# Attention on one Trainium2 core: block moves in a VectorE form with an accumulator, and five buffers in place of three

## The chip, the cores and the metric

The kernel runs on one core of a Trainium2 chip. The metric is the time of one execution in microseconds (us) of device time. The engines of the core work side by side and each takes its own instructions in order: TensorE (PE, with its weight loads shown as PEld), VectorE (DVE), ScalarE (ACT), GpSimd (POOL) and SyncE (SP, which issues the DMAs here). They wait for one another through semaphores.

## The reference

Softmax attention without a mask, for 16 x 32 = 512 heads; each head has 192 queries and 1024 keys of 128 elements, all in bf16.

```python
B, H, Sq, Sk, D = 16, 32, 192, 1024, 128
def reference(q, k, v):
    scale = q.shape[-1] ** -0.5
    scores = jnp.einsum("bhqd,bhkd->bhqk", q, k) * scale
    p = _softmax(scores, axis=-1)
    return jnp.einsum("bhqk,bhkd->bhqd", p, v)
```

## The kernel before, in words

The 512 heads are taken in 128 quads of four heads; x counts quads. A quad has three steps, so there are 384 steps (f for the scores, s for the outputs, which run four steps behind: LAG = 4). Per step PE makes a third of the scores of the quad (`qk`, L612) and then a third of the outputs of the quad before (`pv`, L631).

What the engines do for a quad:

- SP loads K (1 MB, into `f_kn`), Q (0.19 MB, `f_qn`) and V (1 MB, `f_vs`), L505, L511 and L519, three buffers each (`NKN`, `NVS`), and stores two quads of outputs at a time (L531).
- DVE transposes K in three pieces into `f_kx` (`turn_k`, L697) and Q into `f_qt` (`turn_q`, L706), in blocks of 32 x 32.
- POOL puts the transposed K in order, in three copies, into `f_kt` (`order`, L570), and copies V in two halves into `f_vp` (`spread`, L579), where each row of 128 elements has a column of ones behind it. `f_kt` and `f_vp` have two buffers.
- PE multiplies K by Q into PSUM (`f_s`), ACT takes exp of it into `f_pt` (L788 and L791), PE multiplies that by V into PSUM (`f_o`); the column of ones gives the sum of the row.
- DVE divides (`onorm`): the reciprocal of the sums (L718), then the product with the outputs (L723).

`f_o` is a single PSUM bank. `pv(s)` therefore takes the semaphore `f_on` once (L627, through `take`, L596), which the product of `onorm(s - 1)` raises: PE cannot begin a step's outputs before DVE has divided those of the step before.

In every second quad (odd x) the first step is "wide" (`wide`, L496): its matmuls have 128 columns of weights instead of two times 64, so the outputs lie on other partitions than the store wants. `onorm` of a wide step writes into a scratch tile `f_ow`, and four moves of 64 partitions x 128 elements (L735) bring the blocks into `f_ob`. One move stands behind the `onorm` of the first step after the wide one, one behind the second, two behind the third (L729). The order on DVE is written out by hand, L758 to L769: per step f, `onorm(f - 5)` with its moves, then `turn_q` where one is due, then `turn_k(f + 5)`.

The order on SP is written out as well, L536 to L555. Per round n it loads K and Q of quad n + 3, then V of quad n + 1, then stores if a store is due. A load of K waits until DVE has transposed the quad that was in the buffer (`f_kx`, L504); a load of V waits for the second of the three output steps of the quad three before (`f_pv`, L518).

POOL takes, per quad, the three copies of K of quad x and then the two of V of quad x - 1 (L584). A copy of V waits for V's landing and for PE to be done with the buffer of `f_vp` that it overwrites (L577, L578).

A second, general path (`_general_path`) runs only if a sum of exponentials left its range; with these inputs it does not.

Of the kernel before, what the change touches and what calls it, by code (L numbers as in the profile page):

```python
# [6 lines left out]
F32 = mybir.dt.float32  # L7
ACT_FN = mybir.ActivationFunctionType
ALU = mybir.AluOpType
# [388 lines left out]
U32 = mybir.dt.uint32  # L398
# [9 lines left out]
def _attention_kernel(nc, q, k, v, out):  # L408
# [4 lines left out]
    NQ = NH // 4  # L413
# [3 lines left out]
    assert NH % 8 == 0 and NQ >= 12  # L417
    NF = 3 * NQ
    LAG = 4
    NKN, NVS, NKT, NVP = 3, 3, 2, 2  # L420
    GQ = 2
    NSO = 3
    VB = 130
# [9 lines left out]
    with ExitStack() as outer:  # L433
# [26 lines left out]
        with ExitStack() as es:  # L460
            def sb(name, shape, dt):
                return es.enter_context(nc.sbuf_tensor(name, shape, dt))
# [15 lines left out]
            pt = sb("f_pt", [128, R, 4, T * SQ], BF16)  # L478
            ob = sb("f_ob", [128, NSO, GQ * 6, D], BF16)
            ow = sb("f_ow", [128, 2, D], BF16)  # L480
            rinv = sb("f_rinv", [128, 2 * NF], F32)
            chk = sb("f_chk", [128, 2 * NF], F32)
            bad = sb("f_bad", [128, 2], BF16)
# [7 lines left out]
            def o_of(s):  # L491
                if NF - 4 <= s < NF - 1:
                    return s3_ps[0][:, s - (NF - 4), :].rearrange("p (u c) -> p u c", u=2)
                return o_ps[:]

            def wide(s):  # L496
                x, i = divmod(s, 3)
                return i == 0 and x % 2 == 1

            @block.sync  # L500
            def _(e):
                def load_k(x):
                    if x >= NKN:
                        e.wait_ge(s_kx, 3 * (x - NKN) + 3)  # L504
                    e.dma_start(  # L505
                        kn[:, x % NKN, :],
                        kf[4 * x:4 * x + 4].rearrange("a (j r) d -> (a j) (r d)", r=32).bitcast(U32),
                    ).then_inc(s_kn[x % NKN], 16)

                def load_q(x):  # L510
                    e.dma_start(  # L511
                        qn[:, x % NKN, :],
                        qf[4 * x:4 * x + 4].rearrange("a (j u) d -> (a j) (u d)", u=6).bitcast(U32),
                    ).then_inc(s_qn[x % NKN], 16)

                def load_v(x):
                    if x >= NVS:
                        e.wait_ge(s_pv, 3 * (x - NVS) + 2 + LAG)  # L518
                    e.dma_start(  # L519
                        vs[:, x % NVS, :, :],  # L520
                        vf[4 * x:4 * x + 4].rearrange("a (m t) d -> m a (t d)", t=T),
                    ).then_inc(s_v[x % NVS], 16)

                def store(i):
                    so = i % NSO
                    x, c = stores[i]
                    if x + c == NQ:
                        e.wait_ge(s_fin, 1)
                    else:
                        e.wait_ge(s_rc, 3 * (x + c) + 2)  # L530
                    e.dma_start(  # L531
                        of[4 * x:4 * x + 4 * c].rearrange("(a x) (p j) d -> (x p) a (j d)", x=2, j=3),
                        ob[:, so, 0:6 * c, :].rearrange("p (a j) d -> p a (j d)", j=3),
                    ).then_inc(s_st[so], 16)

                load_k(0)  # L536
                load_q(0)
                load_k(1)
                load_q(1)
                load_v(0)  # L540
                load_k(2)
                load_q(2)
                si = 0
                for n in range(NQ + 3):
                    if n + NKN < NQ:
                        load_k(n + NKN)
                        load_q(n + NKN)
                    if n + 1 < NQ:
                        load_v(n + 1)
                    if si < len(stores) - 2 and n >= sum(stores[si]) + 2:  # L550
                        store(si)
                        si += 1
                while si < len(stores):
                    store(si)
                    si += 1  # L555
                for so in range(NSO):
                    e.wait_ge(s_st[so], 16 * len(range(so, len(stores), NSO)))
# [121 lines left out]
            def _(dve):  # L679
# [31 lines left out]
                def onorm(s):  # L711
                    x, w = divmod(s, 3)
                    i, a = where[x]
                    so = i % NSO
                    ri = rinv[:, 2 * s: 2 * s + 2]
                    dve.wait_ge(s_pv, s + 1 + LAG)
                    O = o_of(s)
                    dve.reciprocal(ri, O[:, :, 128]).then_inc(s_rc, 1)  # L718
                    dve.wait_ge(s_rc, s + 1)
                    if a == 0 and w == 0 and i >= NSO:  # L720
                        dve.wait_ge(s_st[so], 16 * (i // NSO))
                    dst = ow[:] if wide(s) else ob[:, so, 6 * a + 2 * w: 6 * a + 2 * w + 2, :]
                    dve.tensor_tensor(  # L723
                        dst,
                        O[:, :, 0:128],
                        ri.unsqueeze(2).to_broadcast([128, 2, D]),
                        ALU.mult,
                    ).then_inc(s_on if s < NF - 1 else s_fin, 1)
                    for back, parts in ((1, (0, 1, 2, 3)),) if s == NF - 2 else ((1, (0,)), (2, (1,)), (3, (2, 3))):  # L729
                        if s == NF - 1 or s < back or not wide(s - back):  # L730
                            continue
                        i, a = where[(s - back) // 3]
                        for part in parts:
                            z, y = divmod(part, 2)
                            dve.tensor_copy(  # L735
                                ob[64 * z: 64 * z + 64, i % NSO, 6 * a + y, :].bitcast(U32),
                                ow[64 * y: 64 * y + 64, z, :].bitcast(U32))

                cnt = [0]

# [17 lines left out]
                for f in range(NF + LAG + 1):  # L758
                    s = f - LAG - 1
                    if s >= 0:  # L760
                        onorm(s)
                        if 0 <= s - EARLY < 3:
                            check(0, 2 * EARLY, 0, s - EARLY)
                    g = f + 5
                    if g < NF:
                        x, b = divmod(g, 3)
                        if b == 2 and x >= 2:
                            turn_q(x)
                        turn_k(g)  # L769
# [26 lines left out]
def bass_standalone__mha_softmax__near_ridge_kernel(  # L796
    nc: bass.Bass,
    q: bass.AP,
    k: bass.AP,
    v: bass.AP,  # L800
    out: bass.AP,
):
    _attention_kernel(nc, q, k, v, out)
# [28 lines left out]
```

## Time and profile before

| | |
|---|---|
| time, median of 3 runs (lowest to highest) | 870.58 us (866.5 to 877.46) |
| the profiled execution: time, span | 875.82 us, 871.8 us |
| granted TensorE clock, mean over the span | 0.99 |
| L735, the moves: count, busy, mean of one | 256, 110.2 us, 430 ns |
| L579, POOL's copies of V: count, mean of one | 256, 1044 ns |
| loads of K, V and Q, issue to landing, median | 10.9, 9.6 and 10.9 us |

The profile is of one execution. Its span runs from the first to the last instruction of the program; the time of the execution is a little longer. Lines are named as L735, line 735 of the kernel. In the list of waits a row has the engine, its tile and line, then behind the arrow what ended the wait, then the total in us, how often, and the longest. PEq is PE's sequencer, the part that takes the instructions and waits for semaphores, and SPq that of SP; "issue" is time in which an engine waited for nothing that the profile shows. In the groups of instructions a row has line, engine, operation, out<-in, sizes (partitions x elements), the count, then busy us, mean ns of one, and the idle time of the engine just before them with what ended it. In the timeline a row has start, length, engine, line, what it does, how many in a row, and in brackets the idle time before it. In the rows of DMA queues the share is the time that packets took on 16 DMA engines.

### The profile page before, as it was taken

To read this page: it belongs to the slowest core of one execution; us is meant where nothing else is said; L and a number is where in the kernel's file an instruction comes from. 1 tells how busy PE (TensorE), PEld (TensorE's weight loads), DVE (VectorE), ACT (ScalarE), POOL (GpSimd) and SP (SyncE) were. 2 spreads that over 40 slices of the span, in tenths; PEclk is the share of its full clock that TensorE was granted. 3 is DMA by queue.
4 is the path that set the end of the run, shared out by engine and by line. 5 is a ranking of instruction groups with operands and counts; after the bars stand their busy time and mean duration, and the time that the engine had idled before them with its cause. 6 is when DMAs were issued, how large, how long until landed. Compare 5 with 4: busy or idle time off the path is not lost. (4 is left out here: it accounts for less than half of the span.)

```text
span 871.8 us, 69465 instructions
## 1 busy us (share of the span) xinstructions
PE 828.7 (95%) x31882; PEld 737.8 (85%) x31882; DVE 707.3 (81%) x1544; ACT 753.2 (86%) x770; POOL 562.5 (65%) x646
## 2 busy tenths in 40 slices
PE   7899999999999999999999999999999999999995
PEld 4788888888888888888889888888888888888885
DVE  5488888888888888888888888888888888888874
ACT  4698988999898889998889888988888888888884
POOL 7466666676666666766666766666666666666661
PEclk9899999999999999999999999999999999999998
DMA  9799999999999999999999999999999999999982
GB/s 360 261 356 398 361 375 403 367 383 404 386 392 381 374 369 391 397 390 375 373 369 398 392 352 393 363 381 381 376 365 405 365 385 375 353 391 376 362 291 80
DMA packets 138303, 319.23 MB, mean 366 GB/s; under 512 B 7184, under 2 KB 56336, under 8 KB 121872
## 3 DMA queue, kind: packets, MB, share of 16 engines
q1 hardware_dynamic: 138256, 318.80, 98.4%
q14 instruction: 41, 0.34, 0.1%
q8 instruction: 6, 0.10, 0.1%
HBM read 293.60 MB, written 25.17 MB: 366 GB/s over the span
## 5 line engine op out<-in xcount | busy, mean ns | idle before, releaser
L791 ACT ACTIVATE f_pt<-f_s 128x1536 bf16<-128x1536 f32 x384 | 555.7, 1447 | 14.4 <-PE f_o L631 14.3
L631 PE MATMUL f_o<-f_vp,f_pt 128*64 128x129 bf16 (+1 forms) x11296 | 432.3, 222 | 24.4 <-PEq L596 23.9
L570 POOL COPY f_kt<-f_kx 128x896 uint32<-128x896 uint32 (+2 forms) x384 | 297.4, 785 | 215.1 <-DVE f_kx L697 143.5
L612 PE MATMUL f_s<-f_qt,f_kt 32*128 32x192 bf16 (+2 forms) x20480 | 425.0, 227 | 8.7 <-issue 5.6
L631 PEld LDWEIGHTS f_o<-f_vp,f_pt 128*64 128x64 bf16 (+1 forms) x11296 | 373.1, 109 | 69.8 <-issue 51.5
L612 PEld LDWEIGHTS f_s<-f_qt,f_kt 32*128 32x128 bf16 x20480 | 359.2, 92 | 49.6 <-issue 14.2
L697 DVE STREAM_TRANSPOSE f_kx<-f_kn 128x896 uint32<-128x896 uint32 (+2 forms) x384 | 334.4, 871 | 12.5 <-DMA f_kn<-in_k_dram 5.9
L579 POOL COPY f_vp<-f_vs 128x1024 uint32<-128x1024 uint32 x256 | 259.8, 1044 | 78.4 <-DMA f_vs<-in_v_dram 65.1
L788 ACT ACTIVATE f_pt<-f_s 128x512 bf16<-128x512 f32 x384 | 229.8, 598 | 91.3 <-PE f_s L612 74.8
L718 DVE RECIPROCAL f_rinv<-f_o 128x2 f32<-128x2 f32 x381 | 62.3, 164 | 124.0 <-PE f_o L631 122.3
L723 DVE TENSOR_TENSOR f_ob<-f_o,f_rinv 128x256 bf16<-128x256 f32 x318 | 135.0, 425 | 10.9
L735 DVE COPY f_ob<-f_ow 64x64 uint32<-64x64 uint32 x256 | 110.2, 430 | 4.8
L706 DVE STREAM_TRANSPOSE f_qt<-f_qn 128x384 uint32<-128x384 uint32 x128 | 72.3, 565 | 0.0
L723 DVE TENSOR_TENSOR f_ow<-f_o,f_rinv 128x256 bf16<-128x256 f32 x63 | 26.8, 425 | 2.2
L664 PE MATMUL f_o<-f_ones 128*128 128x512 bf16 x24 | 7.4, 479 | 1.1 <-POOL f_ones L561 1.1
L664 PEld LDWEIGHTS f_o<-f_ones 128*128 128x128 bf16 x24 | 2.7, 118 | 5.2 <-issue 2.7
L562 POOL MEMSET f_vp<- 128x8320 bf16 x1 | 7.0, 7037 | 0.0
L680 DVE MEMSET f_pt<- 128x3072 uint32 x1 | 2.6, 2618 | 1.5 <-PEq L817 1.5
L631 PE MATMUL f_s<-f_vp,f_pt 128*64 128x129 bf16 (+1 forms) x80 | 3.2, 220 | 0.3 <-PEq L596 0.3
L631 PEld LDWEIGHTS f_s<-f_vp,f_pt 128*64 128x64 bf16 (+1 forms) x80 | 2.9, 107 | 0.6 <-issue 0.4
L780 ACT ACTIVATE f_pt<-f_ones 128x3072 f32<-128x3072 bf16 x1 | 2.8, 2764 | 0.0
L780 ACT ACT_TABLE_LOAD x1 | 1.3, 1283 | 0.8 <-PEq L817 0.8
(16 smaller groups left out, 6.0 us busy)
## 6 DMA issues: line engine op xcount, KB each, us to landing
f_kn<-in_k_dram SPq DMA_DIRECT2D x128, 1024.0 KB, 10.9
f_vs<-in_v_dram SPq DMA_DIRECT2D x128, 1024.0 KB, 9.6
f_qn<-in_q_dram SPq DMA_DIRECT2D x128, 192.0 KB, 10.9
out_dram<-f_ob SPq DMA_DIRECT2D x63, 384.0 KB, 9.8
out_dram<-f_ob SPq DMA_DIRECT2D x2, 192.0 KB, 2.0
```

What stands on the lines that cost most here:

```text
L570: gp.tensor_copy(kt[:, x % NKT].bitcast(U32).rearrange("p U (j s u) c -> p U j s (u c)", s=2, u=2)[:, lo:hi], kx[:, x % 2].rearrange("p (U ...
L579: gp.tensor_copy(vp[:, x % NVP, 2 * T * i: 2 * T * i + 2 * T, 0:D].bitcast(U32), vs[:, x % NVS, 2 * i: 2 * i + 2, :].rearrange("p a (t d) ...
L612: ins = pe.matmul(S[:, c0: c0 + n1 - n0], kt[r, x % NKT, 2 * t + h, :, c], qt[r, x % R, h, n0:n1, c], start=w == 0, stop=w == 3, tile_posi ...
L631: return pe.matmul(O[m0: m0 + m, u, 0:129], pt[:, x % R, 2 * y + z, t * SQ + n0: t * SQ + n0 + m], vp[:, x % NVP, (2 * y + z) * T + t, 0:129],
L664: pe.matmul(o_ps[:].rearrange("p a b -> p (a b)"), ones[:], ones[:].unsqueeze(1).to_broadcast([128, 4, 128]), start=True, stop=True)
L697: dve.transpose(kx[:, x % 2].rearrange("p (U s j u) -> p s u U j", s=2, j=32, u=2)[:, :, :, lo:hi], kn[:, x % NKN].rearrange("p (s u U i) ...
L706: dve.transpose(qt[:, x % R].bitcast(U32).rearrange("p b (y j u) c -> p u y b (j c)", y=3, u=2), qn[:, x % NKN].rearrange("p (u y b i) -> ...
L718: dve.reciprocal(ri, O[:, :, 128]).then_inc(s_rc, 1)
L723: dve.tensor_tensor(dst, O[:, :, 0:128], ri.unsqueeze(2).to_broadcast([128, 2, D]), ALU.mult,).then_inc(s_on if s < NF - 1 else s_fin, 1)
L735: dve.tensor_copy(ob[64 * z: 64 * z + 64, i % NSO, 6 * a + y, :].bitcast(U32), ow[64 * y: 64 * y + 64, z, :].bitcast(U32))
L788: act.activation(pt[:, x % R, 0, c], s1_ps[:], ACT_FN.Exp, scale=scale).then_inc(s_e1, 1)
L791: act.activation(pt[:, x % R, 1:4, c], s3_ps[f % 2][:], ACT_FN.Exp, scale=scale).then_inc(s_e3, 1)
```

## The change

Two things are changed. The four moves per pair of quads are made by `tensor_scalar` in place of `tensor_copy`: the block is read as 128 elements of bf16 instead of 64 words of 32 bits, multiplied by 1.0, and the maximum of each partition's elements is written out besides, into a new tile `f_junk` that nobody reads. And K, Q and V have five buffers each; to use them, SP loads five quads of K and Q and three of V ahead, and in each round V (of quad n + 3) stands before K and Q (of quad n + 5).

```diff
-    NKN, NVS, NKT, NVP = 3, 3, 2, 2
+    NKN, NVS, NKT, NVP = 5, 5, 2, 2
...
+            junk = sb("f_junk", [128, 4], F32)
...
-                load_v(0)
-                load_k(2)
-                load_q(2)
+                for n in range(2, NKN):
+                    load_v(n - 2)
+                    load_k(n)
+                    load_q(n)
                 si = 0
                 for n in range(NQ + 3):
+                    if n + NKN - 2 < NQ:
+                        load_v(n + NKN - 2)
                     if n + NKN < NQ:
                         load_k(n + NKN)
                         load_q(n + NKN)
-                    if n + 1 < NQ:
-                        load_v(n + 1)
                     if si < len(stores) - 2 and n >= sum(stores[si]) + 2:
...
-                            dve.tensor_copy(
-                                ob[64 * z: 64 * z + 64, i % NSO, 6 * a + y, :].bitcast(U32),
-                                ow[64 * y: 64 * y + 64, z, :].bitcast(U32))
+                            dve.tensor_scalar(
+                                ob[64 * z: 64 * z + 64, i % NSO, 6 * a + y, :],
+                                ow[64 * y: 64 * y + 64, z, :], 1.0, None, ALU.mult, ALU.max,
+                                accum_out=junk[64 * z: 64 * z + 64, part: part + 1])
```

On SP, in the steady part, the loads and the store of one pair of quads stood like this before:

```order
L505 DMA f_kn<-in_k_dram 128x2048 [waits f_kx]
L511 DMA f_qn<-in_q_dram 128x384
L519 DMA f_vs<-in_v_dram 128x4x1024 [waits f_pv]
L505 DMA f_kn<-in_k_dram 128x2048 [waits f_kx]
L511 DMA f_qn<-in_q_dram 128x384
L519 DMA f_vs<-in_v_dram 128x4x1024 [waits f_pv]
L531 DMA out_dram<-f_ob 128x4x384 [waits f_rc]
```

and now like this:

```order
L520 DMA f_vs<-in_v_dram 128x4x1024 [waits f_pv]
L506 DMA f_kn<-in_k_dram 128x2048 [waits f_kx]
L512 DMA f_qn<-in_q_dram 128x384
L520 DMA f_vs<-in_v_dram 128x4x1024 [waits f_pv]
L506 DMA f_kn<-in_k_dram 128x2048 [waits f_kx]
L512 DMA f_qn<-in_q_dram 128x384
L532 DMA out_dram<-f_ob 128x4x384 [waits f_rc]
```

V, which waits for PE, has moved ahead of the K and Q of its round, so that these now follow its wait; the store stands behind Q instead of behind V. The line numbers are one higher here, from `junk` on, and two higher behind the loads.

On DVE, behind the wide step (its product writes `f_ow`), the rows before were:

```order
L723 TENSOR_TENSOR f_ow<-f_o,f_rinv 128x256 [waits f_rc]
L697 STREAM_TRANSPOSE f_kx<-f_kn 128x2x2x6x32 [waits f_qk]
L718 RECIPROCAL f_rinv<-f_o 128x2 [waits f_pv]
L723 TENSOR_TENSOR f_ob<-f_o,f_rinv 128x256 [waits f_rc]
L735 COPY f_ob<-f_ow 64x64
L706 STREAM_TRANSPOSE f_qt<-f_qn 128x2x3x2x32 [waits f_qk,f_qn0]
L697 STREAM_TRANSPOSE f_kx<-f_kn 128x2x2x3x32 [waits f_qk]
L718 RECIPROCAL f_rinv<-f_o 128x2 [waits f_pv]
L723 TENSOR_TENSOR f_ob<-f_o,f_rinv 128x256 [waits f_rc]
L735 COPY f_ob<-f_ow 64x64
```

and now are:

```order
L725 TENSOR_TENSOR f_ow<-f_o,f_rinv 128x256 [waits f_rc]
L699 STREAM_TRANSPOSE f_kx<-f_kn 128x2x2x6x32 [waits f_qk]
L720 RECIPROCAL f_rinv<-f_o 128x2 [waits f_pv]
L725 TENSOR_TENSOR f_ob<-f_o,f_rinv 128x256 [waits f_rc]
L737 TENSOR_SCALAR f_ob,f_junk<-f_ow 64x128
L708 STREAM_TRANSPOSE f_qt<-f_qn 128x2x3x2x32 [waits f_qk,f_qn1]
L699 STREAM_TRANSPOSE f_kx<-f_kn 128x2x2x3x32 [waits f_qk]
L720 RECIPROCAL f_rinv<-f_o 128x2 [waits f_pv]
L725 TENSOR_TENSOR f_ob<-f_o,f_rinv 128x256 [waits f_rc]
L737 TENSOR_SCALAR f_ob,f_junk<-f_ow 64x128
```

Nothing on DVE has changed its place; the moves have another operation, twice the number of elements and a second output.

## The prediction

> **What bounds the kernel now.** I read the page's busy times first, then the waits, then the windows, and last the timeline of one stretch.
>
> ```profile
> PE 828.7 (95%) x31882; PEld 737.8 (85%) x31882; DVE 707.3 (81%) x1544; ACT 753.2 (86%) x770; POOL 562.5 (65%) x646
> q1 hardware_dynamic: 138256, 318.80, 98.4%
> HBM read 293.60 MB, written 25.17 MB: 366 GB/s over the span
> ```
>
> Two things look full: PE at 95% and the DMA queue at 98.4%. The share of the queue cannot decide between them, because loads go out as soon as a buffer is free and the queue therefore always holds something. The waits say more.
>
> ```profile
> PEld f_o L631 <- issue: 51.5, 164, 1.3
> PE f_o L631 <- PEq L596: 23.9, 56, 1.1
> POOL f_vp L579 <- DMA f_vs<-in_v_dram: 65.1, 86, 1.6
> DVE f_kx L697 <- DMA f_kn<-in_k_dram: 5.9, 2, 4.2
> ```
>
> PE's idle time stands ahead of its P·V matmuls (L631), at the take of a semaphore (L596). V's landing is waited for by POOL only, and K's landing, apart from the start, by nobody. I then cut the steady part at the starts of the P·V of wide steps (128 columns of weights, one in every two quads, so one pair of quads lies between two cuts). Two stretches of five pairs each, and the last stage:
>
> ```profile
> 256.33:323.26 66.93, 63.87 (x2486) 56.99 (x2481) 57.19 (x121) 58.76 (x60) 44.26 (x51) 1.00 1.02 378
> 323.26:386.51 63.25, 63.14 (x2485) 56.69 (x2481) 51.91 (x121) 58.23 (x60) 42.69 (x50) 1.00 1.03 391
> 849.27:871.80 22.53, 13.65 (x471) 12.26 (x466) 9.78 (x33) 9.70 (x10) 3.19 (x4) 0.86 0.28 89
> ```
>
> The columns are length, busy time of PE, PEld, DVE, ACT and POOL with counts, granted clock, DMA share, GB/s. The same work took 66.93 us in one stretch, 13.39 a pair, and 63.25 in the next, 12.65 a pair. In the second PE is busy for 63.14 of 63.25 us: nothing is left to gain there. PE, ACT and POOL spent the same or nearly the same in both. Only DVE differs, by 5.3 us, and the row that makes it up is the move of L735 (the first row is of the slow stretch, the second of the quick one, the third of all 61 pairs from 49.83 to 849.27, four moves to a pair):
>
> ```profile
> L735 DVE COPY f_ob<-f_ow 64x64 uint32<-64x64 uint32 x20 | 11.4, 572 | 0.4
> ...
> L735 DVE COPY f_ob<-f_ow 64x64 uint32<-64x64 uint32 x20 | 5.3, 266 | 0.4
> ...
> L735 DVE COPY f_ob<-f_ow 64x64 uint32<-64x64 uint32 x244 | 107.1, 439 | 4.6
> ```
>
> The timeline of the slow stretch shows how a move of 64 words per partition takes so long and how it reaches PE:
>
> ```profile
> 302.26 2.04 POOL L579 COPY f_vp<-f_vs 128x1024 uint32<-128x1024 uint32 x2 [0.17 <-DMA f_vs<-in_v_dram]
> 302.43 0.92 DVE L735 COPY f_ob<-f_ow 64x64 uint32<-64x64 uint32 x1
> 303.36 1.11 DVE L697 STREAM_TRANSPOSE f_kx<-f_kn 128x896 uint32<-128x896 uint32 x1
> 304.40 0.13 DVE L718 RECIPROCAL f_rinv<-f_o 128x2 f32<-128x2 f32 x1
> 304.56 0.42 DVE L723 TENSOR_TENSOR f_ob<-f_o,f_rinv 128x256 bf16<-128x256 f32 x1
> 305.02 1.09 DVE L735 COPY f_ob<-f_ow 64x64 uint32<-64x64 uint32 x2
> 305.08 0.98 POOL L570 COPY f_kt<-f_kx 128x896 uint32<-128x896 uint32 x1 [0.79 <-PE f_s L612]
> 305.13 1.12 PE L631 MATMUL f_o<-f_vp,f_pt 128*64 128x129 bf16 x32 [0.19 <-PEq L596]
> 306.12 0.98 DVE L697 STREAM_TRANSPOSE f_kx<-f_kn 128x768 uint32<-128x768 uint32 x1
> 307.19 0.42 DVE L723 TENSOR_TENSOR f_ob<-f_o,f_rinv 128x256 bf16<-128x256 f32 x1
> 307.76 1.11 PE L631 MATMUL f_o<-f_vp,f_pt 128*64 128x129 bf16 x32 [0.42 <-PEq L596]
> ...
> 862.71 0.79 DVE L735 COPY f_ob<-f_ow 64x64 uint32<-64x64 uint32 x4
> ```
>
> The move of 302.43 begins inside POOL's two copies of V and ends at 303.35, with the first of the two (half of 2.04 after 302.26). The pair of moves from 305.02 ends at 306.11, 0.05 behind POOL's copy of K. At the end of the program, with POOL idle, four moves took 0.79, about 0.2 each. So a move waits until POOL's copy in hand is over. DVE's queue is in order: behind the late move stand a transpose (L697) and then the next normalization (L718, L723), and PE may not overwrite its one bank of outputs before that is done. PE's matmuls begin 0.15 after each late L723, at 305.13 and 307.76. The kernel is therefore bound by PE at 12.65 a pair, plus what the moves' waits for POOL push through DVE: (849.27 - 49.83) / 61 = 13.11 a pair on the mean.
>
> **The new form of the move.** Before, 64 words; now 128 elements of 2 bytes, multiplied by 1.0, with a running maximum that is written to f_junk. Four per pair, 256 in all, in the same places. Is the wait for POOL gone? No row of this trace has this form, so the bounds are 0 and the whole wait. The rows say only that the copy waits and that the transposes, the other DVE work on SBUF, do not: L697's 1.11 at 303.36 lies beside POOL's copy and is no longer than its usual time (next fence). The Trainium skill, SBUF — State Buffer, section Who interferes with whom, says that copies and tensor_scalar can enter modes that lock the port pair shared with GpSimd, for the whole instruction, but not the tensor_scalar form that also writes out its accumulator; the trace agrees with the first half (572 ns beside POOL, about 200 without), no row here shows the second. I take the wait as gone, since one instruction form that leaves POOL's port alone exists in the trace already.
>
> The form's own price:
>
> ```profile
> L697 DVE STREAM_TRANSPOSE f_kx<-f_kn 128x896 uint32<-128x896 uint32 x128 | 141.9, 1109 | 11.6 <-DMA f_kn<-in_k_dram 5.9 <-PE f_s L612 4.8
> L718 DVE RECIPROCAL f_rinv<-f_o 128x2 f32<-128x2 f32 x381 | 62.3, 164 | 124.0 <-PE f_o L631 122.3
> L748 DVE TENSOR_REDUCE f_bad<-f_chk 128x1 bf16<-128x750 f32 x1 | 0.9, 936 | 0.0
> L748 DVE TENSOR_REDUCE f_bad<-f_chk 128x1 bf16<-128x18 f32 x1 | 0.2, 175 | 0.0
> L744 DVE TENSOR_SCALAR f_chk<-f_rinv 128x18 f32<-128x18 f32 x1 | 0.2, 166 | 0.0
> ```
>
> The nearest rows are L744, the same operation on 18 elements, 166 ns, and the slope of a reduction, (936 - 175) / (750 - 18) = 1.04 ns an element. 128 elements cost 166 + 110 x 1.04 = 280 if one goes per step, and no less than the idle-POOL move's 0.79 / 4 = 198 if more do. Writing the accumulator costs nothing at the least, and at most one more small instruction, 164 as L718. So 198 to 444; I take 360, the middle of 280 and 444, because a running maximum resembles the reduction most.
>
> Does 360 reach PE? In the slow stretch the moves took 4 x 572 = 2288 ns a pair and PE lost 13.39 - 12.65 = 0.74. If each ns of late move costs PE one ns, the schedule swallows 2288 - 740 = 1550 a pair, 388 a move. At 4 x 266 = 1064 it swallowed all. 4 x 360 = 1440 lies under 1550: the cover (DVE's idle time ahead of L718, 122.3 us in all) holds, with 28 ns a move to spare. At 444 it is gone and PE pays 4 x 56 = 224 ns a pair, 14 us over 63 pairs.
>
> **The five buffers.** They move no work, only when loads go out. These are the two SyncE waits that pace the loads, and one round of them:
>
> ```profile
> SPq L519 <- PE f_o L631: 431.7, 125, 14.2
> 301.53 0.33 SPq L505 DMA_DIRECT2D f_kn<-in_k_dram  x1
> 306.29 0.38 SPq L519 DMA_DIRECT2D f_vs<-in_v_dram  x1
> ```
>
> In each round V now stands ahead of K and Q, so the wait for P·V (L519) holds back K and Q behind it: K's buffer was free at 301.53 and the load would now follow V, 306.29 - 301.53 = 4.8 us later. But the ring is two quads longer, 12.6 us, so K still goes out 7.8 us earlier against its use, and V 12.6 earlier. A store that waits for a normalization now stands behind all three loads of its round instead of ahead of the next K; its own wait is for the same step. What POOL loses is the 65.1 us of waiting for V; it then waits for a free buffer of f_vp instead. That gains PE nothing by itself: the copy of V at 302.26 to 304.30 serves a P·V that starts at 309.9, more than 5 us later. It does make POOL's copies of V start at their earliest, in the same place of every pair.
>
> The start can go either way:
>
> ```profile
> 22.05 1.44 PE L612 MATMUL f_s<-f_qt,f_kt 32*128 32x192 bf16 x39 [3.32 <-issue]
> 28.73 0.24 PE L612 MATMUL f_s<-f_qt,f_kt 32*128 32x64 bf16 x8 [2.25 <-issue]
> ```
>
> PE idles here within one run of matmuls, waiting for nothing the profile shows, while the first loads are on their way. Now more of them are queued at once. I take no change; the bounds are all 5.6 us gained and 5.6 more lost.
>
> **The sum.** 49.83 us until the first cut, unchanged; 61 pairs at 12.65 = 771.7 in place of 799.4; 22.5 at the end, unchanged: 844.0, that is 27.8 less than the span of 871.8. The execution profiled took 875.82, 4.0 more than its span, so **848.0 us**. That execution lies within the runs of before (866.5 to 877.46) and 0.6% above their median of 870.58. I leave the forecast at 848, since in it no pair depends any more on where POOL's copies happen to fall, which is what differs from pair to pair now. Against the median it is 2.6% less.
>
> **Rivals.**
> 1. The new form is dear. It waits for nobody, but takes 444: the 14 us above, 862 us. For it: the form has two results, and the margin is 28 ns a move. Against: the second result is one value per partition, and at a mean of 266 the moves cost PE nothing at all.
> 2. The DMA becomes the bound, and PE's waits only move. 318.8 MB at 378 GB/s, the rate of the slow stretch, are 843 us; with 3 us before the first packet and some 17 of work after the last load (the last stage's 22.5 less the 5 in which its 2 MB move), 863, or 867 with the 4.0. For it: the share of 98.4%. Against: the quick stretch moved 391 GB/s for 63 us with a share hardly higher, and 12.65 a pair asks for 318.8 / 64 / 12.65 = 394. The Trainium skill's DMA: Bandwidth & Descriptors, section Specifications, gives 368 GB/s as the vendor's derated figure; by it the bytes alone would take an estimated 866 us and this change could bring nothing. The row of 391 contradicts it here.
> 3. The change does not do what it says, and turns out slower: the form waits for POOL as the copy did. With V always there, POOL's copies of V would start at their earliest in every pair, as between 256 and 323, so that every pair would be a slow one: 49.8 + 61 x 13.39 + 22.5 + 4.0 = 893 us. It decides as soon as the moves' mean beside POOL is again near 572. For it: no row here has the form, and it reads and writes the same tiles as the copy. Against: L697 does not wait.
>
> **How the numbers follow.** Forecast 0.65, rival 1 0.15, rival 2 0.12, rival 3 0.08. About 2% is what a measurement of this kernel tells from no change: 853.2 and 888 are the bounds. The forecast falls under 853.2 except for a tenth of it (a start that loses 5.6, a move between 388 and 444); of the rivals 1 and 2 together 0.05 might. Faster 0.64, same 0.28, slower 0.08. The range: below, 848 less a start that gains its 5.6 and a little from the 0.11 us of idle PE in the quick stretch, 841; above, to rival 2, 867, which leaves rival 3 and the ends of the others out.
>
> **What would show it.** The line of the moves as TENSOR_SCALAR, 256 of them, mean between 198 and 390 and none near 1000; the two waits of L631 (51.5 and 23.9) down to a few us, all cuts 12.6 to 12.7 apart, some 390 GB/s in the windows; DVE busy near 707 - 110 + 92 = 689; POOL's 65.1 for V gone. The forecast is wrong if waits ahead of L631 remain with moves that are short (then another engine is late), if moves stay long beside POOL (rival 3), or if POOL or DVE waits for landings while PE idles (rival 2).

## The result, and the profile after

| | before | after |
|---|---|---|
| time, median (lowest to highest of 4 runs each) | 871.5 us (866.5 to 877.46) | 847.38 us (846.71 to 848.63) |
| ratio, with its 95% interval | | 0.972 (0.966 to 0.979) |
| profiled execution: time, span | 875.82, 871.8 us | 847.42, 843.1 us |
| first cut (start of the second pair's wide P·V after the start) | 49.83 us | 48.06 us |
| 61 pairs up to the last cut | 799.4 us, 13.11 a pair | 772.1 us, 12.66 a pair |
| from the last cut to the end | 22.5 us | 22.9 us |

The kernel is 2.8% faster, and its runs lie closer together: 1.9 us apart instead of 11. The page's rows of busy time and of the DMA queue, to be held against the first fence of the prediction:

```profile
PE 824.7 (98%) x31882; PEld 734.7 (87%) x31882; DVE 671.8 (80%) x1800; ACT 748.5 (89%) x770; POOL 560.3 (66%) x646
q1 hardware_dynamic: 138256, 318.80, 99.4%
```

PE's busy time is nearly what it was, on a shorter span. DVE has 256 instructions more, 1800 for 1544, though the program has one row per move as before. The waits show where the time came from (the P·V is now L633, the take L598, POOL's copy of V L581):

```profile
PEld f_o L633 <- issue: 21.5, 131, 0.3
POOL f_vp L581 <- PE f_o L633: 10.6, 3, 5.8
PE f_o L633 <- PEq L598: 0.2, 1, 0.2
```

The 23.9 us of PE ahead of the P·V are gone, and POOL waits no longer for V's landing. (PEld's 51.5 us went down to 21.5, not to the few us that the prediction named; the kernel without any moves, further on, has the same 21.5.) The windows from the first cut to the last, and from there to the end:

```profile
48.06:820.17 772.11, 771.56 (x30260) 691.78 (x30257) 634.67 (x1708) 709.44 (x732) 527.21 (x611) 1.00 1.02 389
820.17:843.10 22.93, 13.67 (x470) 12.28 (x466) 10.30 (x41) 9.69 (x10) 3.19 (x4) 0.85 0.13 39
```

PE is busy for 771.56 of 772.11 us. An idle time of PE below a fifth of a percent, which the kernel before had in its quick stretches only (0.11 of 63.25 us in the prediction's), now holds for the whole steady part. The moves themselves, in the groups (first two rows) and by their shortest, median and longest (third row, ns):

```profile
L737 DVE TENSOR_SCALAR_CACHE_REDUCE f_ob<-f_ow 64x128 bf16<-64x128 bf16 x256 | 71.1, 278 | 4.8
L737 DVE DVE_READ_ACCUMULATOR f_ob<-f_ow 64x1 f32 x256 | 19.7, 77 | 0.0
...
L737 DVE TENSOR_SCALAR_CACHE_REDUCE f_ob<-f_ow x256: 266/281/285, 39.2 to 834.5; 64x128 bf16<-64x128 bf16 x128
```

Each move is two instructions, which explains the 256 more: the move itself, 266 to 285 ns whatever POOL does, and a read of the accumulator, 77 ns. The timeline behind a wide step, the same place as in the prediction (in this and the other timelines below, rows between those shown are left out):

```profile
306.59 2.03 POOL L581 COPY f_vp<-f_vs 128x1024 uint32<-128x1024 uint32 x2
307.03 0.28 DVE L737 TENSOR_SCALAR_CACHE_REDUCE f_ob<-f_ow 64x128 bf16<-64x128 bf16 x1
307.24 0.08 DVE L737 DVE_READ_ACCUMULATOR f_ob<-f_ow 64x1 f32 x1
307.33 1.11 DVE L699 STREAM_TRANSPOSE f_kx<-f_kn 128x896 uint32<-128x896 uint32 x1
308.44 1.10 PE L614 MATMUL f_s<-f_qt,f_kt 32*128 32x128 bf16 x48
309.20 0.28 DVE L737 TENSOR_SCALAR_CACHE_REDUCE f_ob<-f_ow 64x128 bf16<-64x128 bf16 x1
309.42 0.08 DVE L737 DVE_READ_ACCUMULATOR f_ob<-f_ow 64x1 f32 x1
309.47 1.13 PE L633 MATMUL f_o<-f_vp,f_pt 128*64 128x129 bf16 x32
309.50 0.28 DVE L737 TENSOR_SCALAR_CACHE_REDUCE f_ob<-f_ow 64x128 bf16<-64x128 bf16 x1
309.72 0.08 DVE L737 DVE_READ_ACCUMULATOR f_ob<-f_ow 64x1 f32 x1
309.81 0.98 DVE L699 STREAM_TRANSPOSE f_kx<-f_kn 128x768 uint32<-128x768 uint32 x1
```

The move of 307.03 runs through the middle of POOL's copies and takes as long as the one of 309.20, when POOL is idle. The read lies for the most part inside the move's time: from the start of a move to the start of what follows it some 0.30 pass in these rows. PE's matmuls at 309.47 have no idle time ahead of them.

### The profile page after: what moved, and what is told of

Read it like the earlier page. It is cut to its first block, busy times and chain, and to the rows that moved or that the text cites. A ratio compares the mean times of both kernels' runs of the same rounds, so it can differ in the third digit from the quotient of the medians.

```text
span 843.1 us, 69721 instructions
## 1 busy us (share of the span) xinstructions
PE 824.7 (98%) x31882; PEld 734.7 (87%) x31882; DVE 671.8 (80%) x1800; ACT 748.5 (89%) x770; POOL 560.3 (66%) x646
## 5 line engine op out<-in xcount | busy, mean ns | idle before, releaser
L633 PE MATMUL f_o<-f_vp,f_pt 128*64 128x129 bf16 (+1 forms) x11296 | 431.0, 221 | 0.8 <-PEq L598 0.2
L633 PEld LDWEIGHTS f_o<-f_vp,f_pt 128*64 128x64 bf16 (+1 forms) x11296 | 370.2, 109 | 45.1 <-issue 21.5
L581 POOL COPY f_vp<-f_vs 128x1024 uint32<-128x1024 uint32 x256 | 259.6, 1043 | 12.9 <-PE f_o L633 10.6
L720 DVE RECIPROCAL f_rinv<-f_o 128x2 f32<-128x2 f32 x381 | 62.5, 164 | 130.6 <-PE f_o L633 124.7
L737 DVE TENSOR_SCALAR_CACHE_REDUCE f_ob<-f_ow 64x128 bf16<-64x128 bf16 x256 | 71.1, 278 | 4.8
L737 DVE DVE_READ_ACCUMULATOR f_ob<-f_ow 64x1 f32 x256 | 19.7, 77 | 0.0
L633 PE MATMUL f_s<-f_vp,f_pt 128*64 128x129 bf16 (+1 forms) x80 | 3.2, 220 | 0.3 <-PEq L598 0.3
L633 PEld LDWEIGHTS f_s<-f_vp,f_pt 128*64 128x64 bf16 (+1 forms) x80 | 2.9, 107 | 0.5 <-issue 0.4
```

The source lines that it names most:

```text
L581: gp.tensor_copy(vp[:, x % NVP, 2 * T * i: 2 * T * i + 2 * T, 0:D].bitcast(U32), vs[:, x % NVS, 2 * i: 2 * i + 2, :].rearrange("p a (t d) ...
L633: return pe.matmul(O[m0: m0 + m, u, 0:129], pt[:, x % R, 2 * y + z, t * SQ + n0: t * SQ + n0 + m], vp[:, x % NVP, (2 * y + z) * T + t, 0:129],
L737: dve.tensor_scalar(ob[64 * z: 64 * z + 64, i % NSO, 6 * a + y, :], ow[64 * y: 64 * y + 64, z, :], 1.0, None, ALU.mult, ALU.max, accum_out ...
```

## The experiments

Theory going in: the gain is that the move no longer waits for POOL, and the buffers alone bring nothing, or make it worse (the prediction's third rival). All times are medians, of four runs (two for the doubled moves and for Q loaded twice), each with its ratio to the kernel before, timed on the same chip; "pair" is (last cut - first cut) / 61 of the profiled execution, as in the table above.

| kernel | median us | ratio, 95% interval | pair us |
|---|---|---|---|
| new form, three buffers | 847.95 | 0.971 (0.965 to 0.977) | 12.64 |
| old copy, five buffers | 851.17 | 0.975 (0.969 to 0.981) | 12.69 |
| five buffers, no accumulator | 850.93 | 0.975 (0.969 to 0.981) | 12.70 |
| five buffers, no moves | 847.06 | 0.971 (0.965 to 0.977) | 12.65 |
| five buffers, every move twice | 864.89 | 0.989 (0.981 to 0.997) | 12.90 |
| old copy, five buffers, fill 128 | 890.95 | 1.019 (1.012 to 1.025) | 13.36 |
| old copy, five buffers, fill 400 | 904.96 | 1.035 (1.029 to 1.042) | 13.56 |
| old copy, five buffers, fill 520 | 848.76 | 0.973 (0.967 to 0.979) | 12.66 |
| new form, five buffers, fill 128 | 848.02 | 0.970 (0.964 to 0.976) | 12.64 |
| kernel after, Q loaded twice | 897.83 | 1.030 (1.022 to 1.038) | 13.44 |

**The two parts apart.** First the form alone, on the kernel before:

```diff
-    dve.tensor_copy(ob[...].bitcast(U32), ow[...].bitcast(U32))
+    dve.tensor_scalar(ob[...], ow[...], 1.0, None, ALU.mult, ALU.max, accum_out=junk[...])
```

> The new form of the move alone, with three buffers and the old order of loads. Theory (the gain is the move's wait for POOL, and the buffers move no time): moves of 0.28 us, no wait ahead of P·V that DVE causes, pairs of quads at 12.65 to 12.7 us, 846 to 851 us, with POOL still waiting for V's landings some 65 us. Rival (the three buffers, or the DMA behind them, are a second bound that the slow moves hid): V lands later from pair to pair until PE waits for it, pairs near 12.85 or more, 858 us or more.

It came out as the theory has it. V's landing is waited for longer than ever, and it does not matter:

```profile
L736 DVE TENSOR_SCALAR_CACHE_REDUCE f_ob<-f_ow 64x128 bf16<-64x128 bf16 x256 | 71.1, 278 | 4.8
...
POOL f_vp L580 <- DMA f_vs<-in_v_dram: 163.5, 104, 2.6
```

POOL stands 163.5 us for V, 65.1 in the kernel before (probably because shorter pairs ask for V sooner; this was not looked into); pairs still take 12.64. (The 65 us that I expected here were the figure of the slower kernel.)

Then the buffers alone, on the kernel after:

```diff
-    dve.tensor_scalar(ob[...], ow[...], 1.0, None, ALU.mult, ALU.max, accum_out=junk[...])
+    dve.tensor_copy(ob[...].bitcast(U32), ow[...].bitcast(U32))
```

> The five buffers alone, with the old copy as move. Theory: nothing gained, and worse than before, since V is always there, POOL copies it at its earliest in every pair, and the old copy then waits for POOL in every pair as it did between 256 and 323 us of the kernel before: pairs at 13.35 to 13.55, mean of a move near 570 ns, 885 to 895 us. Rival (the landings of V were part of the loss): pairs shorter than 13.1 on the mean and 865 us or less.

Here the theory failed: 851 us, where 885 to 895 were expected. The old copy still waits for POOL, but in every pair in the same way, and less:

```profile
L737 DVE COPY f_ob<-f_ow 64x64 uint32<-64x64 uint32 x256 | 88.2, 344 | 4.8
...
310.40 2.03 POOL L581 COPY f_vp<-f_vs 128x1024 uint32<-128x1024 uint32 x2
310.80 0.69 DVE L737 COPY f_ob<-f_ow 64x64 uint32<-64x64 uint32 x1
311.51 1.11 DVE L699 STREAM_TRANSPOSE f_kx<-f_kn 128x896 uint32<-128x896 uint32 x1
312.17 1.10 PE L614 MATMUL f_s<-f_qt,f_kt 32*128 32x128 bf16 x48
313.17 0.39 DVE L737 COPY f_ob<-f_ow 64x64 uint32<-64x64 uint32 x2
313.28 0.92 PE L633 MATMUL f_o<-f_vp,f_pt 128*64 128x129 bf16 x25
313.41 0.99 POOL L572 COPY f_kt<-f_kx 128x896 uint32<-128x896 uint32 x1 [0.97 <-PE f_s L614]
```

POOL's copies of V start 0.40 ahead of the second move of the pair, so that the move waits only for the rest of the first copy, 0.69 long. In the slow stretch of the kernel before (fence in the prediction) they started 0.17 ahead, at 302.26 for 302.43, and the move took 0.92. That quarter of a microsecond moved the last two moves as well: here they start at 313.17, ahead of POOL's copy of K, and take 0.39 together; there they met it and took 1.09. What is left of the wait shows in PE by 0.08 a pair: the P·V behind that move starts 313.28 - 312.17 = 1.11 after the scores ahead of it, in the kernel after 309.47 - 308.44 = 1.03. 4 x 344 = 1376 ns of moves a pair lie under the 1550 that the prediction had worked out, 4 x 572 above. So I formed a second theory: not whether V is there early, but where POOL's copy lies against the moves, to a few hundredths of a microsecond, decides.

The trace of the kernel before holds the same pair already:

```profile
81.46 2.03 POOL L579 COPY f_vp<-f_vs 128x1024 uint32<-128x1024 uint32 x2
81.85 0.69 DVE L735 COPY f_ob<-f_ow 64x64 uint32<-64x64 uint32 x1
84.22 0.39 DVE L735 COPY f_ob<-f_ow 64x64 uint32<-64x64 uint32 x2
```

Here POOL did not have to wait for V. Sorted by how far POOL's copies of V started ahead of the second move, the 61 pairs of that trace fall apart cleanly: with 0.39 to 0.41, 4 pairs of 12.68 to 12.69; with 0.05 to 0.25, 24 pairs of 13.35 to 13.56; with the copies up to 0.43 behind that move, 23 pairs of 12.60 to 12.70; with the copies still later, so that the last two moves meet them, 10 pairs of 13.35 to 13.83. With the old copy and five buffers the lead is 0.37 to 0.41 in all 61 pairs. In the slow stretch the copy of 302.26 had waited 0.17 for V's landing, as the bracket of its row in the prediction says: that was not yet POOL's earliest place.

**Is it the accumulator?** The kernel after with the accumulator left out of the move:

```diff
-    ow[...], 1.0, None, ALU.mult, ALU.max, accum_out=junk[...])
+    ow[...], 1.0, None, ALU.mult)
```

> The kernel after, but the move's tensor_scalar has no accumulator: the same bf16 operands and multiplication. Theory (it is the accumulator that keeps the move off what POOL's copy holds; the Trainium skill, SBUF — State Buffer, section Who interferes with whom, names this difference): the moves wait for POOL again, mean 500 ns or more, pairs at 13.3 to 13.5, 880 to 895 us. Rival (the operation or the 2-byte elements make the difference, not the accumulator): moves below 300 ns without a wait and 845 to 849 us.

```profile
L737 DVE TENSOR_SCALAR f_ob<-f_ow x256: 176/193/697, 39.6 to 837.1; 64x128 bf16<-64x128 bf16 x128
```

The mechanism is as expected, the time is not: the move waits again, up to 697 ns, exactly as the old copy does in the same kernel (mean 344 for both, pairs of 12.70 and 12.69), and so costs as little as that does. Operation and element size are therefore not what frees the move from POOL; the accumulator is. The Trainium skill, SBUF — State Buffer, section Who interferes with whom, exempts just this form from the lock on the port pair shared with GpSimd; these rows agree, 697 without the accumulator and at most 285 with it.

**Does anything of the moves still cost PE time?** The kernel after with the moves taken out:

```diff
-    dst = ow[:] if wide(s) else ob[:, so, 6 * a + 2 * w: 6 * a + 2 * w + 2, :]
+    dst = ob[:, so, 6 * a + 2 * w: 6 * a + 2 * w + 2, :]
...
-    for part in parts:
-        ...
+    pass
```

> The kernel after without the four moves: the product of a wide step is written straight into the output tile, so blocks of every second quad's first step are stored in the wrong places. Theory (PE is the bound in the kernel after, and the moves lie wholly in DVE's idle time): 846 to 849 us, pairs at 12.65. Rival (the moves still cost PE something, through the product of the next step): pairs at 12.58 to 12.62, 842 to 845 us.

```profile
DVE f_rinv L720 <- PE f_o L633: 208.6, 381, 5.3
```

847.06 for 847.38: nothing. The moves' time is now DVE's idle time; it waits for PE ahead of all 381 reciprocals, 208.6 us instead of 124.7.

**How much cover is there?** Every move made twice, the second time into a tile that is not stored:

```diff
+    dve.tensor_scalar(od[64 * z: 64 * z + 64, part, :], ow[64 * y: 64 * y + 64, z, :],
+                      1.0, None, ALU.mult, ALU.max, accum_out=junk[..., 4 + part: 5 + part])
```

> The kernel after with every move made twice, the second time into a tile that is not stored (eight moves per pair). Theory (the schedule swallows about 1550 ns of moves a pair, and each ns above costs PE one): 8 x 280 = 2240, so PE loses 0.69 us a pair, pairs near 13.35, 885 to 895 us, and the waits ahead of P·V are back although no move waits. Rival (what PE lost before was POOL's doing and not lateness of DVE as such): pairs below 12.9, 862 us or less.

The direction is the theory's: no move waits (277 ns mean), and yet PE loses time to DVE again, 0.24 a pair. The size is not: 0.69 was expected, nearly three times that, and the time, 865 us, lies between the two forecasts, nearer to the rival's 862. The timeline of the last two moves shows a part of the reason:

```profile
304.34 0.28 DVE L738 TENSOR_SCALAR_CACHE_REDUCE f_ob<-f_ow 64x128 bf16<-64x128 bf16 x1
304.55 0.08 DVE L738 DVE_READ_ACCUMULATOR f_ob<-f_ow 64x1 f32 x1
304.55 0.28 DVE L742 TENSOR_SCALAR_CACHE_REDUCE f_od<-f_ow 64x128 bf16<-64x128 bf16 x1
304.76 0.08 DVE L742 DVE_READ_ACCUMULATOR f_od<-f_ow 64x1 f32 x1
304.85 0.98 DVE L700 STREAM_TRANSPOSE f_kx<-f_kn 128x768 uint32<-128x768 uint32 x1
...
306.49 1.11 PE L634 MATMUL f_o<-f_vp,f_pt 128*64 128x129 bf16 x32 [0.23 <-PEq L599]
```

The second of two moves on the same partitions starts 0.21 after the first, inside its recorded 0.28; what follows stands 0.30 behind it. Counted from start to start a doubled move takes 0.51, not 0.56, and the first of a pair less (the transpose that follows it starts with its last read). So the eight moves hold DVE for less than the 2.24 us that the forecast added up. The other part is where PE waits: only ahead of the P·V behind the last two moves (62 times, 14.5 us in all, that is 0.24 a pair), so what is left unused ahead of the earlier P·V does not help there. The cover was counted in recorded durations and for the pair as a whole, so it was a rough figure; it did say on which side of the edge the kernel lies.

**Does the place of POOL's copy decide?** POOL fills a tile that nobody reads, ahead of each quad's copies of V; only the length of the fill differs:

```diff
     gp.wait_ge(s_pv, 3 * (x - NVP) + 3 + LAG)
+    gp.memset(idle[:, x % 4, :], 1.0)
```

With the old copy as move and 128 elements:

> Five buffers and the old copy as move, and POOL fills a tile that nobody reads, 128 elements, 0.21 us, just before each quad's two copies of V, so that these start 0.2 us later. In the five-buffer kernel with the old copy, POOL's V copy of the second quad of a pair starts 5.56 us after the wide step (the same in every pair), the second move stands at 5.95 and waits 0.5 us, and the last two moves, at 8.3, run free. Theory (it is the place of POOL's copy against the moves that decides): at 5.8 the second move waits for nearly the whole copy, about 0.9 us long, PE and DVE slip, the last moves meet POOL's copy of K, and pairs take 13.3 to 13.6: 880 to 895 us. Rival (the early landings as such did it): 0.2 us of POOL's idle time cost nothing, 849 to 855 us.

This came out as expected, 891 us and pairs of 13.36: POOL's copy starts 0.25 ahead of the second move, which takes 0.84, and the last two meet the copy of K. With 400:

> The same with 400 elements in the fill, about 0.44 us, so POOL's V copy would start near 6.0 us, just behind the second move. Theory: the second move goes first and takes 0.2, the last two stand at 8.1 behind the end of POOL's copies near 8.05: pairs back at 12.65, 846 to 853 us, faster with the longer delay than with the shorter. Rival (any delay of POOL's copies costs, the more the longer): 885 us or more.

This did not: 905. Its timeline says why:

```profile
301.03 2.03 POOL L583 COPY f_vp<-f_vs 128x1024 uint32<-128x1024 uint32 x2
301.06 1.06 DVE L739 COPY f_ob<-f_ow 64x64 uint32<-64x64 uint32 x1
301.37 1.13 PE L635 MATMUL f_o<-f_vp,f_pt 128*64 128x129 bf16 x32
303.66 0.97 POOL L573 COPY f_kt<-f_kx 128x896 uint32<-128x896 uint32 x1 [0.60 <-PE f_s L616]
303.79 1.10 DVE L739 COPY f_ob<-f_ow 64x64 uint32<-64x64 uint32 x2
303.90 1.13 PE L635 MATMUL f_o<-f_vp,f_pt 128*64 128x129 bf16 x32 [0.38 <-PEq L600]
```

POOL's copy began 0.03 ahead of the move, not behind it, and the move had to wait for all of it, 1.06. This alone would fit the rival, that a longer delay simply costs more. So the fill was made longer still, 520 elements:

> Five buffers, the old copy as move, and a fill of 520 elements ahead of POOL's copies of V. With 400 elements these copies started at 5.92 us after the wide step, 0.03 ahead of the second move at 5.95, so the move waited for a whole copy and pairs took 13.56. By the two fills so far (128: 5.70, 400: 5.92) 520 elements put them at 6.02, just behind the second move's start. Theory (the place decides): the second move goes first and takes 0.2, the last two at 8.1 meet at most the end of POOL's copies: pairs at 12.65 to 12.75, 846 to 856 us, 50 us less than with the shorter fill. Rival (a longer delay of POOL costs more): 905 us or more.

```profile
309.16 0.19 DVE L739 COPY f_ob<-f_ow 64x64 uint32<-64x64 uint32 x1
309.23 2.03 POOL L583 COPY f_vp<-f_vs 128x1024 uint32<-128x1024 uint32 x2
311.30 0.40 DVE L739 COPY f_ob<-f_ow 64x64 uint32<-64x64 uint32 x2
311.77 1.84 POOL L573 COPY f_kt<-f_kx 128x896 uint32<-128x896 uint32 x2 [0.51 <-PE f_s L616]
```

Now the move goes first and takes 0.19, the last two stand behind the end of POOL's copies, and the kernel takes 849 us. A shift of 0.1 us of one copy on an engine that is idle a third of the time is worth 56 us (1.035 of the kernel before with the one fill, 0.973 with the other). The rival is out. And the same shift under the new form:

> The kernel after with the same fill of 128 elements ahead of POOL's copies of V. Theory (the new form does not care where POOL's copies lie): moves of 0.28 us, pairs at 12.65, 846 to 849 us, as without the fill. Rival (POOL itself gets late by the fill): pairs longer than 12.75, 853 us or more.

848.02, where the old copy takes 890.95 with the same fill. The form takes the place out of the matter.

**How near is the DMA's own bound?** Each Q is loaded a second time, into a tile that nobody reads:

```diff
+    if x >= NKN:
+        e.wait_ge(s_qw[x % NKN], 16 * (x // NKN))
+    e.dma_start(qw[:, x % NKN, :], qf[4 * x:4 * x + 4]...).then_inc(s_qw[x % NKN], 16)
```

> The kernel after, in which each Q is loaded a second time into a tile that nobody reads: 25.2 MB more, 344.0 MB in all, 5.375 MB a pair. Theory (the DMA has little room above the 391 to 394 GB/s that pairs of 12.65 ask for; the best fortieths of the span moved 406): it becomes the bound at 395 to 406 GB/s, pairs at 13.2 to 13.6, 880 to 905 us, with waits for landings ahead of POOL or DVE. Rival (there is room): 344.0 / 64 / 12.65 = 425 GB/s are moved and the time stays at 846 to 850 us.

```profile
100.00:800.00 700.00, 658.79 (x25748) 590.03 (x25740) 534.83 (x1454) 603.65 (x623) 446.63 (x519) 1.00 1.04 397
...
DVE f_ob L733 <- DMA out_dram<-f_ob: 53.4, 51, 1.5
DVE f_kx L707 <- DMA f_kn<-in_k_dram: 52.2, 99, 4.7
PE f_o L641 <- PEq L606: 45.5, 54, 1.5
```

The DMA moved 397 GB/s over 700 us and no more; DVE waits for landings of K and for stores, and PE waits for DVE. The kernel after, over the same stretch:

```profile
100.00:800.00 700.00, 699.49 (x27428) 627.10 (x27416) 575.54 (x1548) 643.13 (x665) 477.24 (x553) 1.00 1.03 394
```

It asks for 394 (the 389 up to its last cut count time in which the loads are already through). So it stands some 1% under its next bound, as far as the 397, measured with the added loads among the others, holds for its own loads too.

## Why the prediction was right, and where it was wrong

The time was right (848.0 for 847.38), and so were the three terms: the start 49.8 for 48.1, the pairs 771.7 for 772.1, the end 22.5 for 22.9; the profiled execution took 4.3 more than its span for 4.0. The start lies between 48.1 and 51.0 us in all the kernels above, with three buffers and with five, so its difference from before says nothing of the buffers; and since it alone varies by 2.9, that the total came within 0.7 is in part luck.

- **What bounds the kernel** (PE at 12.65, plus what late moves push through DVE) held: taking the moves out altogether gains nothing over the kernel after, doubling them loses 0.24 a pair without any wait for POOL.
- **The form leaves POOL alone**: held, and it is the accumulator that does it.
- **Its price**: forecast 360, within 198 to 444. Measured 278, and 0.30 from start to start with the read. The middle of 280 and 444 was too much: the read of the accumulator, counted at up to 164, is 77 and lies mostly inside the move. The 280, worked out from a reduction of f32 elements, nearly is the 278 of the move; no run shows that this is more than luck.
- **The cover of 388 a move**: the right side, not the right size, as the doubled moves show; and it is not one cover for the pair, since PE waits step by step.
- **That the five buffers gain PE nothing by themselves**: wrong. Alone they bring the old copy to 851 us. What failed is the step behind it, that POOL's copies of V, when at their earliest, lie where they lay between 256 and 323 us, and with it the third rival's 893: they come 0.2 us earlier than there, and at that place the moves cost little. The row of 302.26, with its 0.17 of waiting for V, and the pair at 81.46 could have shown it beforehand. The 893 is not wrong as a price, only as a place: with a fill of 128 elements the same kernel takes 891.
- **The sum is right although that step is wrong**, because the two parts remedy one fault: the form takes away the wait, and the buffers take away the spread in POOL's starts that made the wait long in some pairs. Either nearly suffices, and together they are worth no more than the form alone (847.4 and 848.0, the intervals overlap). But the buffers alone suffice only by the place that they give POOL's copies: 0.15 us later, with the fill of 128, the same kernel takes 40 us more.
- **The DMA as bound**: rightly put below the forecast, but its price was wrong. 378 GB/s, the rate of the slow stretch, was what was asked for, not what can be had; 397 can, and by it the rival's own sum gives 827.

What stays open: with the old copy PE still loses 0.08 a pair to the move of 0.69, but its pairs are longer by 0.04 only (12.69 for 12.66). The kernel after loses the other 0.04 one step earlier: from the scores to the P·V ahead of that one 1.11 pass on the mean, with the old copy 1.08; why is not known. Whether it is the two more buffers or the new order of the loads that keeps POOL's starts together was not taken apart. And that the new form alone is as good as both together is shown only as far as the intervals go.

## What to carry to other kernels

When instructions of one engine wait for another engine's, look at where the two lie against each other, not at how busy the engines are: 0.1 us of shift on a third-idle engine moved this kernel by 56 us. Two stretches of one trace that do the same work in different times give the gain of a change and its bound, before it is made; all pairs sorted by the suspected cause give more, here that the buffers alone would help. And a change of two parts is not understood until each has been run alone; here each part by itself gives nearly the whole.

## What the runs showed of the hardware

- `tensor_scalar` with an accumulator runs beside POOL's copies at 266 to 285 ns for 64 x 128 bf16; without it the same block takes 193 at the median and up to 697 beside POOL, and the copy of 64 words up to 1.08 us (with the fill of 400). The form that is slower when nothing disturbs it is the better one here.
- With the old copy, a move that starts 0.03 us behind a copy of POOL waits for all of it (1.06); one that starts 0.07 ahead does not wait at all (0.19).
- One core's DMA held 397 GB/s for 700 us with packets of 768 bytes to 8 KB, 1536 bytes those of the added loads.
